# A new order of operations for the first two token chunks, with fixed buffer slots and two steps in halves

## The chip, the cores and the metric

One core of a Trainium2 chip runs the whole kernel. The core has a matrix engine (TensorE, PE in the views; its weight loads are PEld), VectorE (DVE), ScalarE (ACT), GpSimd (POOL), and SyncE (SP), whose queue issues all transfers between HBM and the on-chip memory SBUF. Matrix results go to PSUM, eight banks of 128 x 512 floats. The metric is the device time of one execution in microseconds.

## The reference, cut to what matters

Four sequences of 768 tokens, 8 heads of 64, all float32. Each query sees keys less than 16 positions away, and one summary for each block of 32 tokens (maximum of the keys, mean of the values). Its result is the input of a two-layer network.

```
k_sum = k.reshape(B, H, nb, 32, D).max(axis=3);  v_sum = v.reshape(B, H, nb, 32, D).mean(axis=3)
scores_l = scale * q @ k.T, -1e9 outside |i - j| < 16
scores_s = scale * q @ k_sum.T + log(32)
a = softmax(concat(scores_l, scores_s));  x = a @ concat(v, v_sum)      # 3072 tokens x 512
out = square(relu(x @ w_in)) @ w_out                                     # 512 -> 2048 -> 512
```

## The kernel before, in words

The 3072 tokens are 24 groups `g` of 128; two groups make a chunk `c`, so there are 12 chunks. The hidden width of 2048 is cut into 16 slices `f` of 128. For each chunk and slice, `ffn1` (L382) makes 12 matrix products of 256 columns: x and the weights are each split into a high and a low part, and three of the four pairs are multiplied. `ffn2` (L429) multiplies the squared result by the second weights, three products for each of two groups, 512 columns wide or as two of 256.

From chunk 2 on, the order is a plain loop (`slot`, `period`), in which the attention of the next chunk runs under the layers of this one. The change doesn't touch it. Chunks 0 and 1 are ordered by `START`, a list of tokens that stands in the file; one loop (L646 to L655) goes through it and issues each step to its engine's queue. Every engine works its queue in order. So the list sets, for each engine alone, what stands behind what, on SP too. The scheduler adds the semaphore waits that the data need, and no other freedom is left. The tokens that the prediction speaks of:

- `L:kv` (keys of sequence 0, for two heads each), `L:q`, `L:k`, `L:v`, `L:vn` (values for the means), `L:mask` (constants), `L:w` (weights, whole or a half): loads on SP.
- `KS` (L180): maximum over blocks of 32 keys, on DVE. `S` (L285, and L269 for groups 4 on): scores. `TT` (L297, DVE): mask and maximum of one head. `E` (L305, ACT): exponentials of one head. `NR`, `N` (L318, L325): sums, and division on POOL. `T` (L331, PE) and `TC` (L126): transposes of four heads, and their copy to SBUF.
- `SV` (L149, PE): block means of the values as products with a small matrix; `VC` (L126): copies of a quarter of them beside the loaded values, in the tiles `v_sb0` and `v_sb1`. `O` (L352): output of the attention. `XH`, `XL` (L366, L369): its high and low part.
- `HI`, `LO`, `SH`, `AD`, `CA`, `SU` (L229 to L254): turn a block of 64-bit weights into a high and a low float part, on ACT, DVE and POOL.
- `F1`, `F2`: a slice of the first layer; a slice of the second. `RE`, `SQ`, `MU`, `GL`: square of the relu and its low part. `Z` (L563): products of zeros whose result nobody reads.

Large blocks (keys, raw weights, split weights) lie in rooms of 32 KB per partition. Before, one pool of 18 rooms deals them out in turn:

```
def room(dtype, name):
    return big.tile([P, 8192 // mybir.dt.size(dtype)], dtype, name=name, tag="w", bufs=NF + SPARE)
```

Of the kernel before, what the change touches and what calls it, by code (L numbers as in the profile page):

```python
# [68 lines left out]
GL15v O5=4 VT3 F2.14.1 XH5 XL5
"""  # L70


# [1 line left out]
def attn_ffn_kernel(ctx: ExitStack, tc: tile.TileContext, q, k, kt, v, vt, v0, w, consts, out):  # L74
    nc = tc.nc
# [3 lines left out]
    big = ctx.enter_context(tc.tile_pool(name="big", bufs=1))  # L79
# [59 lines left out]
    def load_v(g):  # L139
        nc.sync.dma_start(out=v_sb[g % 2][0:96], in_=v[g // NT, g % NT])  # L140

    def sum_v0(vn):


        ps = ps_o.tile([P, DM], F32, name="o_ps")
        for t in range(NT):
            o = 20 - 4 * t
            for j in range(4):
                nc.tensor.matmul(  # L149
                    ps[j * 32 : j * 32 + 32, 0:P], lhsT=mean_sb[:, o : o + 32],  # L150
                    rhs=vn[t // 3][:, t % 3, j * P : (j + 1) * P], start=(t == 0), stop=(t == NT - 1),
                )
        return ps
# [10 lines left out]
    def load_kv0(p):  # L164


        if (p // 2) not in padded:
            padded[p // 2] = r = room(F32, "kv")[:, 0 : 2 * KPAD].rearrange("p (a k) -> p a k", a=2)
            nc.gpsimd.memset(r[:, :, 0:WINDOW], 0.0)
            nc.gpsimd.memset(r[:, :, KPAD - WINDOW :], 0.0)  # L170
        kv[0, p] = padded[p // 2][:, p % 2, WINDOW : WINDOW + S]
        nc.sync.dma_start(out=kv[0, p], in_=kt[0, p])

    def load_kv(b, p):
        kv[b, p] = r = room(F32, "kv")
# [70 lines left out]

    def high_w(f, j, eng):
        if f not in w_sb:
            w_sb[f] = room(F32R, "w_sb").rearrange("p (h c) -> p h c", h=2)
# [319 lines left out]
    def begin(op, i, j, eng, at, after):  # L569
# [167 lines left out]
```

## Time and profile before

| | us |
|---|---|
| runs shown | 606.45, 606.64 (median), 610.62 |
| the profiled execution | 607.6 |
| its span, from the first to the last instruction | 605.8 |
| PE busy, of the span | 593.8 |
| DVE, ACT, POOL busy | 386.0, 265.8, 105.2 |

The profiled execution took 1.8 us more than its span, and 1.0 us more than the median. The span is one timeline; "busy" is the time in which at least one instruction of the engine was under way. The groups of rows below are cut from the page of this execution and from answers on its trace; in a timeline row the first number is the start, the second the length of the merged piece, and brackets give the idle time before it and what ended it.

### The profile page before, as it was taken

What the parts mean: (1) busy time and instruction counts of PE and PEld (TensorE: products, weight loads), DVE (VectorE), ACT (ScalarE), POOL (GpSimd) and SP (SyncE); (2) the same over time, 40 slices, a digit from 0 to 9 for tenths busy, and PEclk for the clock granted to TensorE, in tenths of its full rate; (3) what the DMA queues carried; (4) which work ended last, traced back from release to release, by engine and by line L of the source; (5) the groups of instructions that cost most, each with busy time, mean ns of one, the idle gap of its engine ahead of it and who ended that gap; (6) DMA issues with size and microseconds to landing.
All of it is one profiled execution on the core that took longest, in us unless ns stands there. A gap on an engine that the chain in (4) does not pass through costs nothing.

```text
span 605.8 us, 14834 instructions
## 1 busy us (share of the span) xinstructions
PE 593.8 (98%) x6178; PEld 572.8 (95%) x6178; DVE 386.0 (64%) x1063; ACT 265.8 (44%) x687; POOL 105.2 (17%) x97
## 2 busy tenths in 40 slices
PE   7799999999999999999999999999999999999997
PEld 5689999999999999999999999999999999999997
DVE  5789899777637837847545855865663763663221
ACT  4888884334253432433425325425424434422222
POOL 3745755211100101102101101002101010110000
PEclk9999999999999999999999999999999999999999
DMA  8999571350007006006005204202201400200000
GB/s 274 328 363 417 204 260 56 112 168 35 1 11 269 2 2 226 2 2 226 2 1 199 81 2 131 97 2 87 88 2 38 139 2 2 88 1 2 36 1 35
DMA packets 19890, 60.46 MB, mean 100 GB/s; under 512 B 2288, under 2 KB 2288, under 8 KB 18288
## 3 DMA queue, kind: packets, MB, share of 16 engines
q1 hardware_dynamic: 19824, 59.53, 28.0%
q8 instruction: 48, 0.79, 0.6%
q14 instruction: 18, 0.15, 0.1%
HBM read 53.23 MB, written 6.29 MB: 98 GB/s over the span
## 4 chain that ended last, share of the span: by engine, by line
PE 95%; DMA 3%; DVE 1%; ACT 0%; issue 0%; SPq 0%
PE o_ps L429 43%; PE ph L382 39%; PE s_ps L382 4%; PE ph L352 4%; PE s_ps L269 3%; DMA v_sb<-in_v 1%; DMA q_sb<-in_q 1%; DMA kv<-in_kt 1%; DVE v_sb L126 1%; PE s_ps L285 0%; PE o_ps L149 0%; PE o_ps L563 0%; PE ph L331 0%; PE ph L285 0%; PE s_ps L352 0%
## 5 line engine op out<-in xcount | busy, mean ns | idle before, releaser
L382 PE MATMUL ph<-xh,w_sb 128*128 128x256 f32 x1376 | 241.2, 278 | 0.5 <-DVE xl L369 0.5
L429 PE MATMUL o_ps<-w_sb,gh 128*128 128x256 f32 (+1 forms) x1428 | 237.5, 285 | 0.0
L382 PEld LDWEIGHTS ph<-xh,w_sb 128*128 128x128 f32 x1376 | 213.3, 188 | 8.7 <-issue 1.3
L429 PEld LDWEIGHTS o_ps<-w_sb,gh 128*128 128x128 f32 x1428 | 191.0, 188 | 0.5 <-issue 0.3
L382 PE MATMUL ph<-xl,w_sb 128*128 128x256 f32 x688 | 190.5, 277 | 0.0
L429 PE MATMUL o_ps<-w_sb,gl 128*128 128x256 f32 (+1 forms) x670 | 150.5, 294 | 0.0
L401 DVE TENSOR_TENSOR ph<-ph,r 128x512 f32<-128x512 f32 x85 | 59.3, 699 | 141.5 <-ACT r L390 140.7
L390 ACT ACTIVATE r<-ph 128x512 f32<-128x512 f32 x84 | 49.9, 594 | 189.3 <-PE ph L382 189.3
L382 PEld LDWEIGHTS ph<-xl,w_sb 128*128 128x128 f32 x688 | 129.2, 188 | 0.0
L338 DVE STREAM_TRANSPOSE pT<-e_sb 32x256 f32<-32x256 f32 x240 | 104.6, 436 | 4.1 <-POOL e_sb L325 0.7
L305 ACT ACTIVATE e_sb<-e_sb,nmx 128x120 f32<-128x120 f32 x192 | 73.7, 386 | 75.5 <-DVE nmx L297 75.5
L429 PEld LDWEIGHTS o_ps<-w_sb,gl 128*128 128x128 f32 x670 | 104.6, 188 | 0.4
L325 POOL TENSOR_TENSOR e_sb<-e_sb,total 128x480 f32<-128x480 f32 x47 | 46.2, 991 | 322.1 <-DVE total L319 150.4
L396 ACT ACTIVATE gh<-r 128x512 fp32r<-128x512 f32 x94 | 59.5, 633 | 12.1 <-PE o_ps L429 6.5
L404 DVE TENSOR_TENSOR gl<-ph,gh 128x512 fp32r<-128x512 f32 x85 | 58.8, 692 | 9.2 <-DVE ph L401 0.5
L297 DVE CUSTOM_DVE_ANT_0 e_sb<-s_ps,consts_sb 128x120 f32<-128x120 f32 x180 | 40.7, 277 | 1.9 <-PE ph L331 1.1
L245 POOL TENSOR_TENSOR w_raw<-w_raw 128x1024 int32<-128x1024 int32 (+1 forms) x20 | 35.9, 1800 | 24.7 <-DVE w_raw L234 8.6
L305 ACT ACTIVATION_READ_ACCUMULATOR e_sb<-e_sb,nmx 128x1 f32 x192 | 36.3, 189 | 0.0
L369 DVE TENSOR_TENSOR xl<-ph,xh 128x512 fp32r<-128x512 f32 x22 | 15.2, 691 | 23.3 <-ACT xh L366 23.2
L382 PE MATMUL s_ps<-xh,w_sb 128*128 128x256 f32 x160 | 28.6, 279 | 0.0
L366 ACT CAST xh<-ph 128x512 fp32r<-128x512 f32 x22 | 12.9, 586 | 33.1 <-PE ph L352 33.1
L352 PEld LDWEIGHTS ph<-pT,v_sb 128*64 128x64 f32 x704 | 21.7, 138 | 5.2 <-issue 3.8
(79 smaller groups left out, 412.5 us busy)
## 6 DMA issues: line engine op xcount, KB each, us to landing
w_raw<-in_w SPq DMA_DIRECT2D x12, 1024.0 KB, 13.1
v_sb<-in_v SPq DMA_DIRECT2D x24, 384.0 KB, 4.4
k_sb<-in_k SPq DMA_DIRECT2D x20, 384.0 KB, 6.1
q_sb<-in_q SPq DMA_DIRECT2D x24, 256.0 KB, 5.5
kv<-in_kt SPq DMA_DIRECT2D x16, 384.0 KB, 5.9
out<-ob SPq DMA_DIRECT2D x24, 256.0 KB, 2.0
kv<-in_vt SPq DMA_DIRECT2D x12, 384.0 KB, 6.4
w_raw<-in_w SPq DMA_DIRECT2D x8, 512.0 KB, 8.3
```

Source lines behind the costliest of these rows:

```text
L245: nc.gpsimd.tensor_tensor(out=lo, in0=hi, in1=lo, op=ALU.add)
L297: nc.vector.tensor_tensor_reduce(out=e_sb(g)[:, h, 0:NK], in0=s_ps[g, half][h % 2][:, h // 2, 0:NK], in1=m, scale=-scale, scalar=3.0e38, o ...
L305: nc.scalar.activation(e, e, AF.Exp, bias=nmx[g, half][:, i : i + 1], scale=-1.0, accum_out=sm[g, half][:, i, 0:1])
L325: eng.tensor_mul(out=e, in0=e, in1=sm.pop((g, half)).unsqueeze(2).to_broadcast([P, 4, NK]))
L338: nc.vector.transpose(out=pT[g % 2][j * 32 : j * 32 + 32, :, i * 32 : i * 32 + 32], in_=e_sb(g)[i * 32 : i * 32 + 32, :, j * 32 : j * 32 + ...
L352: nc.tensor.matmul(xp[o : o + 64, h // 2, s * 64 : s * 64 + 64], lhsT=v_sb[g % 2][:, s, h * 64 : h * 64 + 64], rhs=pT[g % 2][:, h, s * 64 ...
L382: nc.tensor.matmul(ph, lhsT=w_sb[f][:, w, cc * P : (cc + 1) * P], rhs=x[c][:, cc, :], start=(n == 0), stop=(n == 3 * NC4 - 1))
L390: nc.scalar.activation(r, ph, AF.Relu)
L396: nc.scalar.activation(gh, r, AF.Square)
L401: nc.vector.tensor_mul(out=ph, in0=ph, in1=r)
L404: nc.vector.tensor_sub(out=gl, in0=ph, in1=gh.bitcast(F32))
L429: nc.tensor.matmul(o_ps[c][tt][:, o : o + step], lhsT=g_[:, ts_], rhs=w_sb[f][:, w, DM + o : DM + o + step], start=start and o == 0, stop= ...
```

## The change

`START` is another list of much the same tokens, 508 for 506. Every room has its own name now, and tables of numbers say which block lies in which. The constants are loaded in two parts: the masks of the first two kinds (`L:mask`), and later the third mask, the identity and the small matrix of the means (`L:rest`). `SV` is cut into `SV0` and `SV1`, one for each of the two loads that it reads.

```diff
+RAW_ROOM = (3, 2, 6, 9, 12, 14, 16, 17, 0, 1, 12, 7, 0, 3, 12, 7)
+W_ROOM = (5, 4, 10, 11, 13, 15, 8, 9, 2, 6, 16, 1, 17, 0, 3, 12)
+KV0_ROOM, VN_ROOM, KV_FIRST, KV_ROOM = (0, 1), (7, 8), (14, 14, 7, 17), (7, 14)
...
 START = """
-Z15 XT L:q0 L:kv0 L:kv1 KS0 L:kv3 KS1 L:kv2 KS3 S0.0=01 Z6 L:mask KS2 TT0.3 S0.1=23 TT0.1 L:q1 TT0.0 L:w0.1 L:w1.1
...
+L:kv0 Z15 Z6 L:q0 L:kv1 KS1 KS0 S0.0=01 L:kv3 KS3 L:kv2 KS2 L:mask TT0.2 TT0.0 E0.2 E0.0 TT0.3 E0.3 L:q1 PK5v S0.1=23
...
-    def sum_v0(vn):
-
-
-        ps = ps_o.tile([P, DM], F32, name="o_ps")
-        for t in range(NT):
+    def sum_v0(vn, n, ps):
+        if n == 0:
+            ps = ps_o.tile([P, DM], F32, name="o_ps")
+        for t in range(n * NT // 2, (n + 1) * NT // 2):
...
-    def room(dtype, name):
-
-        return big.tile([P, 8192 // mybir.dt.size(dtype)], dtype, name=name, tag="w", bufs=NF + SPARE)
+    def room(dtype, name, n):
+
+        return big.tile([P, 8192 // mybir.dt.size(dtype)], dtype, name=name, tag=f"room{n}")
...
-            w_raw[f] = room(I64, "w_raw")
+            w_raw[f] = room(I64, "w_raw", RAW_ROOM[f])
...
-            nc.sync.dma_start(out=consts_sb, in_=consts)
+            nc.sync.dma_start(out=consts_sb[:, 0 : 2 * NK], in_=consts[:, 0 : 2 * NK])
+        elif what == "rest":
+            nc.sync.dma_start(out=consts_sb[:, 2 * NK :], in_=consts[:, 2 * NK :])
...
-            v_mean[0] = sum_v0([vn[0], vn[1]])
+            v_mean[0] = sum_v0(vn, i, v_mean.get(0))
```

Counted over both lists, the list has as many zero products as before (32), three `LO` more on ACT and three fewer on DVE, three `CA` the other way round, one `SU` more on DVE and one fewer on POOL, two `RE` more on ACT and two fewer on DVE. Five more slices of the second layer stand directly ahead of another, and are therefore issued as twelve products of 256 columns instead of eight of 256 and two of 512.

The order on three engines, at the places that the prediction speaks of. First PE, between the second pair of transposes of group 1 and the first slice of the first layer; L331 are the transposes (e_sb_77 is that of the even groups), L149 the means, L269 the scores of group 4, L352 the outputs of groups 1 and 0. Before:

```order
L331 MATMUL ph<-consts_sb,e_sb_78 128x128 x4
L563 MATMUL o_ps<-zero 128x512
L331 MATMUL ph<-consts_sb,e_sb_77 128x128 x4
L149 MATMUL o_ps<-vn,consts_sb 32x128 x24
L563 MATMUL o_ps<-zero 128x512
L269 MATMUL s_ps<-k_sb_71,q_sb_75 64x120 x16
L352 MATMUL ph<-pT_80,v_sb_74 64x64 x16
L352 MATMUL s_ps<-pT_79,v_sb_73 64x64 x16
L331 MATMUL s_ps<-consts_sb,e_sb_77 128x128 x4
L331 MATMUL ph<-consts_sb,e_sb_78 128x128 x8
L382 MATMUL s_ps<-xh,w_sb 128x256 x2
```

And of the change (two lines of source further down):

```order
L333 MATMUL ph<-consts_sb,e_sb_78 128x128 x4
L151 MATMUL o_ps<-vn,consts_sb 32x128 x24
L333 MATMUL ph<-consts_sb,e_sb_77 128x128 x4
L354 MATMUL ph<-pT_80,v_sb_74 64x64 x16
L354 MATMUL s_ps<-pT_79,v_sb_73 64x64 x16
L333 MATMUL s_ps<-consts_sb,e_sb_77 128x128 x4
L333 MATMUL ph<-consts_sb,e_sb_78 128x128 x8
L271 MATMUL s_ps<-k_sb_71,q_sb_75 64x120 x16
L384 MATMUL s_ps<-xh,w_sb 128x256 x2
```

The means have moved ahead of the last transposes of group 0, the two zero products are gone from here, and the scores of group 4 stand behind the outputs, where they stood ahead of them.

Second, the copies of the means into `v_sb`. Before, all eight stand together on DVE (L126), behind the sums (L318, L319) of one set of heads and ahead of the sums of another. The change's rows on DVE:

```order
L321 RECIPROCAL total<-total 128x4
L129 COPY v_sb_73<-o_ps 32x2x128
L129 COPY v_sb_74<-o_ps 32x2x128
L129 COPY v_sb_73<-o_ps 32x2x128
L129 COPY v_sb_74<-o_ps 32x2x128
L299 ISA e_sb_77,nmx<-s_ps,consts_sb 128x120
```

and on ACT, with the semaphores that they wait for:

```order
L129 COPY v_sb_73<-o_ps 32x2x128 [waits PE_49]
L129 COPY v_sb_74<-o_ps 32x2x128
L307 ACTIVATE e_sb_78,sm<-e_sb_78,nmx 128x120 [waits DVE_49]
L129 COPY v_sb_73<-o_ps 32x2x128 [waits DVE_49]
L129 COPY v_sb_74<-o_ps 32x2x128
L307 ACTIVATE e_sb_78,sm<-e_sb_78,nmx 128x120
```

Half of the copies have moved to ACT, and the second pair there waits for DVE's first pair; DVE's pairs wait for ACT's in the same way (`VC2a VC0v VC3a VC1v` in the list), so the four pairs follow each other across two engines.

Third, the first loads on SP. Before:

```order
L130 DMA q_sb_75<-in_q 128x512
L172 DMA kv<-in_kt 128x768 x4
L549 DMA consts_sb<-in_consts 128x540
L130 DMA q_sb_76<-in_q 128x512
L218 DMA w_raw<-in_w 128x512 x2
L130 DMA q_sb_75<-in_q 128x512
L218 DMA w_raw<-in_w 128x512
L130 DMA q_sb_76<-in_q 128x512
L547 DMA vn<-in_v 128x1536 x2
```

And of the change:

```order
L174 DMA kv<-in_kt 128x768
L133 DMA q_sb_75<-in_q 128x512
L174 DMA kv<-in_kt 128x768 x3
L551 DMA consts_sb<-in_consts 128x240
L133 DMA q_sb_76<-in_q 128x512
L220 DMA w_raw<-in_w 128x512 x2
L133 DMA q_sb_75<-in_q 128x512
L553 DMA consts_sb<-in_consts 128x300
L133 DMA q_sb_76<-in_q 128x512
L220 DMA w_raw<-in_w 128x512
L549 DMA vn<-in_v 128x1536 x2
```

One load of keys goes ahead of the first queries, and the second part of the constants stands between two loads of queries. On DVE the list puts the reduction of the second pair of heads (`KS1`) ahead of that of the first (`KS0`), which came first before.

## Rows read from the trace of the kernel before

**Rows 1.** The page, parts 1 and 2: PE over the span, granted clock by slice.

```profile
PE 593.8 (98%) x6178; PEld 572.8 (95%) x6178; DVE 386.0 (64%) x1063; ACT 265.8 (44%) x687; POOL 105.2 (17%) x97
...
PEclk9999999999999999999999999999999999999999
```

**Rows 2.** Windows: stretch, its length, busy us by engine, clock, DMA share, GB/s.

```profile
6.00:37.80 31.80, 24.97 (x538) 20.63 (x537) 25.94 (x118) 22.96 (x83) 16.12 (x15) 1.00 0.98 324
30.00:37.80 7.80, 6.76 (x101) 5.97 (x98) 6.99 (x16) 6.29 (x12) 4.59 (x5) 1.00 0.97 306
37.80:60.00 22.20, 22.20 (x206) 21.33 (x203) 20.61 (x47) 19.92 (x29) 11.29 (x7) 1.00 1.02 417
```

**Rows 3.** Waits of PE from 40 us on: us in total, times, longest.

```profile
PE ph L382 <- DVE xl L369: 0.5, 1, 0.5
```

**Rows 4.** Chain that ended last, first 40 us: start, us, what held it.

```profile
1.63 5.60 DMA kv<-in_kt
...
29.46 7.22 DMA v_sb<-in_v
```

**Rows 5.** PE timeline to 38 us: start, us, instructions, idle before and releaser.

```profile
1.18 4.92 PE L563 MATMUL o_ps<-zero 128*128 128x512 f32 x15 [1.18 <-DVE zero L116]
...
18.05 0.40 PE L285 MATMUL s_ps<-kv,q_sb 64*64 64x96 f32 x8 [0.88 <-DMA q_sb<-in_q]
...
21.44 0.63 PE L331 MATMUL ph<-consts_sb,e_sb 128*128 128x128 f32 x4 [0.39 <-DVE pT L126]
21.99 1.51 PE L149 MATMUL o_ps<-vn,consts_sb 128*32 128x128 f32 x46
23.85 0.41 PE L149 MATMUL o_ps<-vn,consts_sb 128*32 128x128 f32 x2 [0.34 <-issue]
25.21 1.05 PE L269 MATMUL s_ps<-k_sb,q_sb 64*64 64x120 f32 x32 [0.54 <-DMA k_sb<-in_k]
...
27.44 0.92 PE L352 MATMUL ph<-pT,v_sb 128*64 128x64 f32 x24 [0.26 <-DVE v_sb L126]
...
33.59 0.33 PE L331 MATMUL ph<-consts_sb,e_sb 128*128 128x128 f32 x1 [0.78 <-issue]
...
36.72 1.15 PE L352 MATMUL ph<-pT,v_sb 128*64 128x64 f32 x32 [0.20 <-DMA v_sb<-in_v]
37.80 0.50 PE L382 MATMUL ph<-xh,w_sb 128*128 128x256 f32 x2
```

**Rows 6.** PE timeline, a piece of the second layer and the instruction behind it.

```profile
45.45 0.40 PE L429 MATMUL o_ps<-w_sb,gl 128*128 128x256 f32 x2
45.69 0.63 PE L429 MATMUL o_ps<-w_sb,gh 128*128 128x256 f32 x3
46.16 0.40 PE L429 MATMUL o_ps<-w_sb,gl 128*128 128x512 f32 x1
46.40 0.40 PE L382 MATMUL ph<-xh,w_sb 128*128 128x256 f32 x2
```

**Rows 7.** DVE timeline: reductions of the keys, first mask step, the mean's copies.

```profile
4.44 0.95 DVE L180 TENSOR_REDUCE ksum<-kv 128x24 f32<-128x768 f32 x1 [3.33 <-DMA kv<-in_kt]
7.25 2.90 DVE L180 TENSOR_REDUCE ksum<-kv 128x24 f32<-128x768 f32 x3 [1.86 <-DMA kv<-in_kt]
10.07 0.27 DVE L297 CUSTOM_DVE_ANT_0 e_sb<-s_ps,consts_sb 128x120 f32<-128x120 f32 x1
...
24.29 3.10 DVE L126 COPY v_sb<-o_ps 32x256 f32<-32x256 f32 x8 [0.69 <-PE o_ps L149]
```

**Rows 8.** ACT timeline: one exponential.

```profile
24.42 0.39 ACT L305 ACTIVATE e_sb<-e_sb,nmx 128x120 f32<-128x120 f32 x1
```

**Rows 9.** DVE timeline: the same subtraction twice.

```profile
73.61 2.92 DVE L254 TENSOR_TENSOR w_sb<-w_raw,w_sb 128x1024 fp32r<-128x1024 f32 x1
...
78.11 1.22 DVE L254 TENSOR_TENSOR w_sb<-w_raw,w_sb 128x1024 fp32r<-128x1024 f32 x1
```

**Rows 10.** POOL timeline at the first of them.

```profile
73.16 2.27 POOL L245 TENSOR_TENSOR w_raw<-w_raw 128x1024 int32<-128x1024 int32 x1 [2.03 <-DVE s_ps L401]
```

More of the change, by code (lines that the diff above doesn't have):

```diff
@@ L69 @@
-GL15v O5=4 VT3 F2.14.1 XH5 XL5
+L:kv0 Z15 Z6 L:q0 L:kv1 KS1 KS0 S0.0=01 L:kv3 KS3 L:kv2 KS2 L:mask TT0.2 TT0.0 E0.2 E0.0 TT0.3 E0.3 L:q1 PK5v S0.1=23
+S1.1=45 TT1.7 TT1.6 E1.6 XT L:w1.1 TT1.5 TT0.1 S1.0=45 TT1.0 PK4v TT1.4 L:w0.1 LO0.1v HI1.1 TT0.6 Z5 SH1.1 CA1.1v E1.0
+E0.1 NR0.0 TT1.2 TT1.1 Z2 N0.0p E1.4 TT0.4 Z2 L:q2 S2.0=12 HI0.1 TT1.3 SH0.1 LO1.1v E1.2 L:rest E1.5 T0.0=0 TT0.7 E1.3
+TT2.3 TT0.5 AD0.1 E1.1 NR1.0 Z1 E1.7 E0.6 Z1 TT2.1 N1.0p T1.0=4 TT2.0 TC0.0v S2.1=12 E0.5 NR1.1 E2.3 L:q3 CA0.1v E0.7
@@ new lines @@
+S3.0=30 TT2.2 TC1.0v TT3.0 TT3.2 L:w2.1 LO2.1a E2.0 HI2.1 N1.1p SH2.1 S3.1=30 E0.4 T1.1=5 L:vn0 E2.2 AD2.1 SV0 L:vn1
+E3.2 SV1 TT3.3 NR0.1 N0.1p T0.1=4 TT3.5 E2.1 E3.0 TT3.4 E3.3 TT3.1 E3.1 TT3.7 E3.4 E3.7 TT3.6 TC1.1v L:v1 NR2.0 VC2a
+VC0v E3.6 VC3a VC1v TT2.4 E3.5 TT2.6 E2.6 O1=5 L:v0 NR3.0 SU0.1p XH1 TC0.1v NR3.1 TT2.5 E2.5 TT2.7 O0=1 XH0 XL1 N2.0p
+T2.0=2 TC2.0a N3.0p T3.0=4 N3.1p T3.1=5 E2.4 XL0 L:k4 L:q4 S4.0=03 L:w3.1 S4.1=03 F1.0.0=1 E2.7 L:v3 AD1.1 SU1.1v
+NR2.1 CA2.1a N2.1p TT4.0 LO3.1a TT4.2 F1.0.1 SU2.1p TC3.0a T2.1=4 HI3.1 SH3.1 CA3.1v AD3.1 RE0v TC3.1a TC2.1a E4.0 SQ0
@@ new lines @@
+O3=2 L:w3.2 HI3.2 XH3 F1.1.0=4 MU0 GL0v TT4.4 TT4.1 LO3.2a TT4.6 SH3.2 XL3 L:v2 O2=5 XH2 SU3.1p XL2 CA3.2a F1.1.1
+L:w0.2 F1.3.0=5 F1.3.1 AD3.2 SU3.2v HI0.2 SH0.2 CA0.2v F1.2.0=2 L:w2.2 L:w1.2 L:w4 LO0.2a LO2.2a F1.2.1 HI2.2 SH2.2
+RE1v HI1.2 SH1.2 CA2.2a AD0.2 SU0.2v AD2.2 LO1.2a F2.0.0 L:k5 E4.1 SQ1 AD1.2 MU1 GL1v CA1.2a SU1.2v SU2.2v L:q5
+S5.1=14 S5.0=14 HI4 SH4 LO4a AD4 TT4.5 TT5.0 TT5.1 TT4.3 RE2v MU2 CA4a E5.0 SU4v L:w5 HI5 F2.0.1 F2.1.0 F2.1.1 SH5
+CA5v LO5a AD5 L:w6 EV0.0v F1.4.0=0 F1.6.0=3 TT5.3 L:q6 SQ2 GL2v EV0.1a HI6 E4.4 SH6 SU5v E5.1 F2.2.0 F2.2.1 L:w7 LO7v
@@ new lines @@
+LO6a HI7 SH7 AD7 RE3a SQ3 TT4.7 E4.6 MU3 TT5.7 GL3v L:w8 HI8 L:w9 L:w11 E5.7 L:q7 F1.4.1 RE4v TT5.4 SQ4 TT5.5 CA6a MU4
+GL4v F1.6.1 E5.4 LO9v AD6 SU6v F2.3.0 F2.3.1 CA7a SU7v F2.4.0 F2.4.1 E4.5 L:w13 TT5.6 TT5.2 HI9 SH9 SH8 LO8a AD8 E5.6
+E4.7 CA8a F1.5.0=2 F1.5.1 RE5v E5.2 RE6a MU5 SQ5 GL5v F1.7.0=5 CA9a L:k7 L:w10 F1.7.1 AD9 MU6 SU8v LO11a SU9v LO10v
+HI10 SH10 F2.5.0 F1.8.0=0 RE7a F1.8.1 HI11 SH11 AD11 E4.2 SQ6 E4.3 GL6v L:kw0 KT0 NR4.0 L:v4 MU7 F2.5.1 EV1.1v EV1.0a
+CA10a L:kw3 VT3 SQ7 L:w12 KT3 AD10 SU10v F1.12.0=1 F1.12.1 GL7p HI13 L:v5 CA11a SU11v SH13 NR4.1 N4.1p LO12a VT0 HI12
@@ new lines @@
+SH12 CA12a RE8v MU8 N4.0p TU4.1 F2.6.0 F2.6.1 SQ8 F2.7.0 F2.7.1 GL8v F1.13.0=2 L:w14 F1.9.0=5 AD12 SU12p HI14 LO13a
+F1.9.1 TU4.0 RE9a MU9 AD13 E5.5 L:w15 SH14 LO14a AD14 L:kw1 CA13a SU13v SQ9 HI15 GL9v KT1 F1.13.1 SH15 CA14a SU14v
+F2.8.0 F2.8.1 F1.14.0=3 F1.10.0=4 F1.10.1 RE10a L:k6 LO15a AD15 E5.3 F1.14.1 F2.9.0 TU4.2 CA15a SU15v SQ10 F2.9.1
+F1.11.0=0 F1.11.1 MU10 RE12a GL10v O4=4 L:kw2 F2.10.0 F2.10.1 RE11v SQ11 MU11 GL11v F2.11.0 NR5.0 N5.0p F2.11.1 KT2
+PK6a NR5.1 RE13a SQ12 MU12 GL12p F1.15.0=5 XH4 EV2.0v F1.15.1 EV2.1v MU13 XL4 N5.1v TU5.1 F2.12.0 SQ13 TU5.0 F2.12.1
@@ L70 @@
+GL13p RE15a MU15 PK7a F2.13.0 F2.13.1 S6.0=01 RE14a SQ14 MU14 SQ15 S7.1=23 S7.0=23 S6.1=01 TU5.2 O5=4 GL14p F2.14.0
+F2.14.1 XH5 VT2 XL5 VT1 GL15v
 """
@@ L174, in load_kv @@
     def load_kv(b, p):
-        kv[b, p] = r = room(F32, "kv")
+        kv[b, p] = r = room(F32, "kv", KV_FIRST[p] if b == 1 else KV_ROOM[p % 2])
         nc.sync.dma_start(out=r[:, 0:S], in_=kt[b, p])
@@ L248, in high_w @@
         if f not in w_sb:
[L249 removed]
+            w_sb[f] = room(F32R, "w_sb", W_ROOM[f]).rearrange("p (h c) -> p h c", h=2)
         copy(eng, w_sb[f][:, 0, part(j)], words(f, j)[1].bitcast(F32))
```

28 lines of the change are left out of this document (2 added, 26 removed).

## The prediction, made before the change was run

> **What bounds the kernel now.** I read the page first. PE is busy 593.8 of 605.8 us and its clock is granted in full in all 40 slices [rows 1]. So nothing can be won by faster neighbours except where PE stands idle, which leaves 12.0 us to find. The windows say where. From 37.80 us on PE has no gap: in the stretch from 37.80 to 60 it is busy 22.20 of 22.20 us [rows 2], and in the waits after 40 us the whole rest of the run shows one, of 0.5 us [rows 3]. From 6.00 to 37.80 PE is busy 24.97 of 31.80, so 6.83 us are idle there [rows 2]; the remaining idle time lies ahead of 6 us, where products of zeros run until the first keys come. The first slice of the first layer, at 37.80 [rows 5], is therefore the milestone (in the change the outputs of group 2, at 36.72 before, stand behind that slice; I count them as work in front of it on both sides): what the change does to the work in front of it (the same work on both sides) goes one for one into the time, and what comes behind it is PE at full load, unless the change opens a gap there.
>
> The chain of waits that ended last begins with the fourth load (keys, from 1.63, landed 7.23) and holds, late, the load of values from 29.46 to 36.68 [rows 4]. Between them the chain hops through all engines. In PE's timeline the reader is to see who released it at each step: transposes at 21.44 waited 0.39 for DVE; the means follow at 21.99; the outputs at 27.44 waited for DVE's copies of those means; the outputs of group 2 at 36.72 waited 0.20 for values. Two pieces waited for nothing that the profile shows, 0.34 at 23.85 and 0.78 at 33.59, marked "issue" [rows 5]. The DMA engines' busy share is 0.98 between 6.00 and 37.80 and 1.02 behind it [rows 2], so one that is put ahead pushes back another.
>
> The sum is made against the profiled execution of 607.6, which is 1.0 above the median of the runs shown, 606.6; I subtract that 1.0 at the end.
>
> **The change part by part.**
>
> *Reductions of the keys, +0.95.* Before, KS0 ran alone at 4.44 for 0.95, in time in which DVE had to wait for keys anyway, and the three others took 2.90 from 7.25, when the later keys landed; the first mask step came at 10.07 [rows 7]. Now KS0 stands behind KS1, whose keys are a later load. DVE works in order, so KS0 falls behind that wait and four stand in a row: the first mask step comes one reduction later, 0.95. If KS1's keys land early, because one load of keys now goes ahead of the queries, nothing is lost. Bounds 0 and +0.95; I take the upper one, as 7.25 is what the row shows for a landing, and the mask steps then feed exponentials, division and transposes one by one.
>
> *Zero products, 0.* There are 32 before and after, 21 of them now at the start. Fifteen took 4.92 us from 1.18 [rows 5], so six more last about 2 us and are over before the four reductions, on which the first scores' masks wait.
>
> *Constants in halves, 0.* Their first part is smaller, but the mask step stands behind KS2 on DVE, which the keys hold, not behind the constants: at 10.07 it follows the reductions with no wait [rows 7]. The second part stands ahead of one load of queries on SP; there PE waited for queries, 0.88 at 18.05 [rows 5]. The same columns are moved in all, the others of them later, so the queries behind them lose what those ahead win. I cost it at nothing.
>
> *Means ahead of the last transposes, -0.94.* PE reached the transposes at 21.44 after 0.39 of waiting, so was free at 21.05. The means began at 21.99 [rows 5]. They wait for no transposes, so they can start at 21.05: 0.94 earlier. Bounds: all of it, or 0 when the values that they read have not landed. No row shows them late, so I take all.
>
> *Copies of the means on two engines, +0.5.* Eight copies in a row took 3.10 on DVE [rows 7], 0.39 each. Now four pairs alternate, ACT, DVE, ACT, DVE, and each waits for the one before, so they do not run beside each other: the 3.10 stays, and three handovers come on top. ACT has an exponential between its pairs, 0.39 [rows 8], beside DVE's pair. A handover from DVE's copy to PE shows as 0.26 [rows 5]. Three of these are 0.8; with the whole exponential in the way 1.2; without any loss 0. I take 0.5, between. DVE is free for two pairs meanwhile, but its next steps wait for products too.
>
> *Scores of group 4, +1.05.* Before, they stood under the copies: PE did them from 25.21 for 1.05 [rows 5], while it would have waited for the copies. Now they stand behind the outputs and transposes, where PE has other work queued, so their 1.05 is on the path, and the place that they filled is idle. Bounds +0.5, if half falls in a gap such as the 0.78 at 33.59, and +1.05, which I take.
>
> *Stalls that go, -1.32.* The 0.20 for values should go, as their loads stand earlier in the list; the two issue gaps lie where PE's program happens to stand, and other instructions stand there now: 0.34 + 0.78 + 0.20 = 1.32 [rows 5]. I take all of it; the other end is -0.30, with a gap of the same kind elsewhere. These gaps are a behaviour of fetching as far as a row can tell: no semaphore ends them. The Trainium skill, *Runtime: NRT & Kernel Launch*, section "Instruction fetch mechanics", says that an engine's program streams in by blocks and that the cost of crossing into the next is mostly hidden. The trace does not bear that out if these gaps are such crossings, 0.34 and 0.78; by the page they would be something else that the change need not remove, and the sum would be 1.12 higher.
>
> *Halved slices of the second layer, 0.* Two products of 256 columns take 0.24 from start to start (45.45 to 45.69), one of 512 takes 0.24 (46.16 to 46.40) [rows 6]. What moves between ACT, DVE and POOL behind 37.80 (three `LO`, three `CA`, one `SU`, two `RE`) is hidden under PE, which shows no gap there; the rooms by table change no duration.
>
> The sum: 0.95 - 0.94 + 0.50 + 1.05 - 1.32 = +0.24, so 607.8 for an execution like the profiled one and **606.8** beside the median. With all low ends (0 - 0.94 + 0 + 0.50 - 1.32 = -1.76) it is 604.9; with all high ends (0.95 + 0 + 1.2 + 1.05 - 0.30 = +2.90) 609.5.
>
> **The rivals.**
>
> *Faster.* The new order may close the gaps in front of the milestone, since every engine's place in line is different. For it speaks that 6.83 us of idle are there and that PE's waits go to many releasers, so one list can serve several. Against it: the loads are at their share throughout, and the keys' landing and the chain through five engines stay. Half of the idle time is 3.4: 606.6 - 3.4 = 603.2. More than 1% (6.1 us) would need nearly all of it.
>
> *Slower, by the clock.* The zero products and the scores that stood between the transposes at 21.44 and the outputs at 27.44 are gone from there. PE then has the means and one set of transposes, and idles until the copies are through, about three pairs of copies, 2.3 us, and more with handovers. The longest idle time before, 0.88 at 18.05 [rows 5], left the granted clock at 1.00 (of 2.4 GHz) in every stretch [rows 2]; nothing shows what a longer one does. If it falls to 1.2 GHz for the products that follow, PE's 6.76 us between 30.00 and 37.80 [rows 2] double at worst, +6.8, or half of them do, +3.4: 606.8 + 3.4 = 610.2 up to 613.6. It decides as soon as the copies start late. The Trainium skill, *TensorE: Matmul & The Clock Gate*, section "HAM oscillation — how this bites in real kernels", has idle gaps of a matmul loop put the engine back to its low clock, so that the next products start cold; it speaks against this change, and the trace of before, with gaps below 0.9 us and a full clock, has no case of it.
>
> *Slower, by thin cover.* Behind 37.80 DVE is busy 20.61 of 22.20 us and ACT 19.92 [rows 2]. The same subtraction on DVE took 2.92 at 73.61 and 1.22 at 78.11; at the first, POOL ran an operation of 2.27 from 73.16 [rows 9, 10]. Such a meeting costs 1.7; if the new order puts one or two where DVE is nearly full, PE waits for it: 606.8 + 1.7 to 3.4 = 608.5 to 610.2.
>
> *No effect.* If a load (the values at 36.68) sets the milestone whatever stands before it, 606.6; this lies in my own range.
>
> **How the numbers follow.** The sum, with no effect, 0.62; faster 0.14; the clock 0.14; thin cover 0.10. The range has to reach into three rivals: 604.2 leaves out the better half of the faster one (0.07), 610.8 the worse part of the clock (0.09), and it takes in 604.9 to 609.5. About 1%, 6.1 us, is what a measurement of this kernel can tell from no change. Faster than 600.5 needs nearly all of the idle time: 0.04. Slower than 612.7 needs most of the clock rival's price, or two rivals together: 0.07. The rest, 0.89, lies within 1%.
>
> **What would show it.** The milestone (first slice with the last outputs) should stand within 38.0 plus or minus 2 us, and PE have no gap behind it. The first mask step should stand near 11.0; the means near 21 to 22; the copies should take 3.1 to 4.3 us from first to last, with PE idle under them for over 2 us; the scores of group 4 should take 1.05 with PE busy on both sides; the gaps marked "issue" should be gone from the means and the transposes. A clock below 1.00 in any stretch, or a wait of PE behind 40 us of more than 1 us, would make the prediction wrong; so would a first mask step ahead of 10 us.

## The result, and the profile after

| | before | the change |
|---|---|---|
| median of 20 runs, us | 606.41 | 610.44 |
| lowest and highest | 605.15 to 610.62 | 607.24 to 615.02 |
| the profiled execution, and its span | 607.6, 605.8 | 609.51, 607.4 |
| ratio, 95% interval | | 1.0069 [1.0055, 1.0083] |

The change is slower by about 4 us, 0.7%. That lies inside the range (604.2 to 610.8) and within 1%, but it is not what the likeliest case said (606.8): it is the rival "slower, by the clock" (610.2 to 613.6). One execution of a variant below (`s4_q4`) ran at a granted clock of 0.56 throughout and took 994.94 us; it is left out of that variant's median, and its trace is the only one of that variant. On the page of the change, TensorE and the clock:

```profile
PE 595.8 (98%) x6188; PEld 576.4 (95%) x6188; DVE 381.1 (63%) x1058; ACT 268.8 (44%) x693; POOL 100.4 (17%) x96
...
PEclk8999999999999999999999999999999999999999
```

PE is busy for 2.0 us more than in [rows 1], though it does no more work worth the name; the first digit of the clock row is 8 where it was 9. Windows show where (the columns are those of [rows 2]):

```profile
6.00:11.90 5.90, 4.44 (x111) 3.55 (x109) 5.10 (x18) 1.44 (x7) 0.00 (x0) 1.00 0.99 363
11.90:15.30 3.40, 3.40 (x37) 2.95 (x36) 2.17 (x14) 2.74 (x11) 0.00 (x0) 0.50 0.51 167
15.30:28.95 13.65, 8.66 (x208) 6.69 (x207) 10.20 (x57) 11.11 (x49) 8.36 (x8) 1.00 0.93 303
28.95:32.37 3.42, 3.42 (x62) 3.30 (x61) 2.45 (x14) 1.65 (x6) 2.66 (x3) 0.50 0.28 67
32.37:60.00 27.63, 27.63 (x321) 26.21 (x320) 22.94 (x54) 24.44 (x47) 14.03 (x11) 1.00 1.02 393
```

Twice, from 11.90 and from 28.95, the granted clock is 0.50 of 2.4 GHz for 3.4 us, with PE busy all through; elsewhere from 6 us on it is full. PE's timeline at the places that the prediction spoke of, to be held against [rows 5]:

```profile
13.06 3.31 PE L567 MATMUL o_ps<-zero 128*128 128x512 f32 x9
16.30 0.40 PE L287 MATMUL s_ps<-kv,q_sb 64*64 64x96 f32 x8
...
19.79 0.65 PE L333 MATMUL ph<-consts_sb,e_sb 128*128 128x128 f32 x4 [1.70 <-POOL e_sb L327]
...
23.81 1.52 PE L151 MATMUL o_ps<-vn,consts_sb 128*32 128x128 f32 x48
25.25 0.33 PE L333 MATMUL ph<-consts_sb,e_sb 128*128 128x128 f32 x1
27.49 0.49 PE L333 MATMUL ph<-consts_sb,e_sb 128*128 128x128 f32 x3 [1.91 <-issue]
27.91 0.34 PE L354 MATMUL ph<-pT,v_sb 128*64 128x64 f32 x4
28.78 1.65 PE L354 MATMUL ph<-pT,v_sb 128*64 128x64 f32 x28 [0.54 <-DVE v_sb L129]
30.21 1.93 PE L354 MATMUL s_ps<-pT,v_sb 128*64 128x64 f32 x32
...
33.66 1.05 PE L271 MATMUL s_ps<-k_sb,q_sb 64*64 64x120 f32 x32
34.64 0.51 PE L384 MATMUL s_ps<-xh,w_sb 128*128 128x256 f32 x2
...
39.10 0.51 PE L384 MATMUL ph<-xh,w_sb 128*128 128x256 f32 x2
...
40.67 1.15 PE L354 MATMUL ph<-pT,v_sb 128*64 128x64 f32 x32
```

In the first stretch nine products of zeros take 3.31 us, and the scores of group 2 stand behind them. Ahead of the second PE does next to nothing for three microseconds: a pause of 1.91 that no semaphore ends, seven short products, then 0.54 of waiting for the copies. What follows runs at half speed: the outputs of group 0 took 1.93 here, where 32 such products took 1.15 in [rows 5]. DVE's and ACT's timelines, for [rows 7]:

```profile
6.19 3.53 DVE L182 TENSOR_REDUCE ksum<-kv 128x24 f32<-128x768 f32 x4 [5.07 <-DMA kv<-in_kt]
9.64 0.27 DVE L299 CUSTOM_DVE_ANT_0 e_sb<-s_ps,consts_sb 128x120 f32<-128x120 f32 x1
...
13.17 0.28 DVE L299 CUSTOM_DVE_ANT_0 e_sb<-ph,consts_sb 128x120 f32<-128x120 f32 x1 [1.16 <-PE ph L287]
...
15.75 0.28 DVE L299 CUSTOM_DVE_ANT_0 e_sb<-s_ps,consts_sb 128x120 f32<-128x120 f32 x1
...
26.52 0.75 DVE L129 COPY v_sb<-o_ps 32x256 f32<-32x256 f32 x2 [0.66 <-ACT v_sb L129]
27.97 0.75 DVE L129 COPY v_sb<-o_ps 32x256 f32<-32x256 f32 x2 [0.70 <-ACT v_sb L129]
```

```profile
25.86 0.63 ACT L129 COPY v_sb<-o_ps 32x256 f32<-32x256 f32 x2
26.52 0.39 ACT L307 ACTIVATE e_sb<-e_sb,nmx 128x120 f32<-128x120 f32 x1
...
27.31 0.63 ACT L129 COPY v_sb<-o_ps 32x256 f32<-32x256 f32 x2 [0.30 <-DVE v_sb L129]
```

Behind 40 us PE waits as it did in [rows 3]:

```profile
PE ph L384 <- DVE xl L371: 0.5, 1, 0.5
```

So PE loses nothing behind it. The prediction's milestone, 37.80, is the start of the second slice of the first layer, not of the first slice (30.83 before, 34.64 in the change). It came at 39.10, and with the 1.08 of the outputs of group 2, which now stand behind it (40.67), at 40.2: 2.4 later than before. Part of that is won back further on. Adding up PE's rows from start to start, up to the same product (the 4,700th from the end, at 136.56 us before and 138.22 after; from there both take 469 us), gives the +1.66 between the two profiled executions by kind of work:

```
outputs +1.19   scores of groups 0 to 3 +0.92   zeros +0.73   transposes +0.65
idle -0.38      means -0.40                     scores of group 4 on -0.23   both layers -0.83
```

PE's idle time did not grow. The four kinds that ran in the two stretches (the first line) grew by 3.5. The two stretches hold 6.8 us of PE's work at half speed, so about 3.4 us of PE's time are the clock's, and all else together fell by 1.7. Two single executions don't bear more than that: the profiled one of before is 1.2 above its kernel's median, that of the change 0.9 below its own. The mean granted clock of each of the 20 runs of the change sorts them:

```
granted clock   runs   us
1.000           2      607.24, 607.74
0.997           1      608.79
0.993, 0.994    12     609.51 to 611.35
0.992, 0.988    2      612.69, 612.76
0.986           3      613.13 to 615.02
```

A stretch of 3.4 us at half clock lowers the mean over 607 us by 3.4 x 0.5 / 607 = 0.003. A mean of 0.999 is a full clock up to PE's last product: in the trace of before the only stretch at 0.50 begins at 604.77, behind it. From row to row the time grows by about 1.4 us for each such stretch, and the typical run has two. That makes some 2.9 of the 4.0 us; about 1 is left at full clock. The kernel before falls too, which its one trace, at full clock, could not show: of all its runs beside the experiments below, 60 have 0.999 or 1.000 (median 606.2) and 26 less (606.8), nearly all of these one stretch. So a fall is rarer there, and by these medians it costs less. These are correlations; the experiments intervene.

### The profile page after: what moved, and what is told of

It is laid out like the page before. It is cut to its first block, busy times and chain, and to the rows that moved or that the text cites. A ratio compares the mean times of both kernels' runs of the same rounds, so it can differ in the third digit from the quotient of the medians.

```text
span 607.4 us, 14853 instructions
## 1 busy us (share of the span) xinstructions
PE 595.8 (98%) x6188; PEld 576.4 (95%) x6188; DVE 381.1 (63%) x1058; ACT 268.8 (44%) x693; POOL 100.4 (17%) x96
## 4 chain that ended last, share of the span: by engine, by line
PE 96%; DVE 1%; DMA 1%; ACT 1%; issue 0%; POOL 0%; SPq 0%; POOLq 0%; DVEq 0%
PE o_ps L431 43%; PE ph L384 39%; PE s_ps L384 5%; PE ph L354 4%; PE s_ps L271 3%; DMA kv<-in_kt 1%; DVE ksum L182 1%; PE o_ps L567 1%; PE s_ps L287 0%; PE s_ps L354 0%; PE ph L333 0%; DVE e_sb L299 0%; PE ph L287 0%; DVE v_sb L129 0%; PE s_ps L333 0%
## 5 line engine op out<-in xcount | busy, mean ns | idle before, releaser
L247 POOL TENSOR_TENSOR w_raw<-w_raw 128x1024 int32<-128x1024 int32 (+1 forms) x20 | 33.1, 1661 | 28.5 <-DVE w_raw L242 17.1
```

The lines of the kernel that those rows point to most:

```text
L247: nc.gpsimd.tensor_tensor(out=lo, in0=hi, in1=lo, op=ALU.add)
```

## The experiments

Theory A: the granted clock. Theory B: the order itself, a longer chain over the copies. Theory C (later): the scores of group 4, whose 1.05 us lost their cover. Each kernel was timed in turn with the kernel before on one chip. Four chips served, on which the kernel before had medians of 606.51 (`zeros_early`, `zeros_long`, `zeros_both`, `before_no_zeros`), 606.00 (`zeros_stall`, `s4_back`, `s4_stall`, `copies_dve`), 606.10 (`after_again`, `before_s4_late`, `s4_q4`) and 606.91 (`before_copies`). So kernels of different groups are compared by their ratios to the kernel before, or by their distance from it, not by their times.

**Five zero products moved forward, `zeros_early`.**

```diff
-L:kv0 Z15 Z6 ... PK5v S0.1=23 ... TT0.1 S1.0=45 ... TT0.6 Z5 SH1.1
+L:kv0 Z15 Z4 ... PK5v Z2 S0.1=23 ... TT0.1 Z3 S1.0=45 ... TT0.6 Z2 SH1.1
```

> The changed kernel with five of its zero products moved into PE's waits: two fewer at the start and three fewer ahead of the scores of group 2, two more ahead of the second scores of group 0 and three more ahead of those of group 1. Theory A (the granted clock): the changed kernel lost time because PE, idle in pieces between 8 and 12 us, was granted half its clock from 11.9 us, and again from 29.0; with the first piece of idle time filled the first fall becomes rarer. It put the nine zeros at 13.06 on the chain at 3.24 us where 2.0 would do, so 1.2 us come back: 609.2, mean granted clock 0.997 instead of 0.994. Theory B (the order): the time went to the longer chain over ACT and DVE in the copies, and the clock only stretches work that waits in any case: 610.4, within 0.4.

Measured: 608.79, ratio 1.0035 [1.0020, 1.0050], below the change's interval. Five of twelve runs had a clock of 1.000 (608.08 to 608.61), six 0.997 (608.71 to 609.86). Theory A gave 609.2; B's 610.4 is out. By the runs the gain is the clock's: at full clock this kernel is no faster than the change (607.24 and 607.74), but more of its runs have it. In its trace the first stretch is gone, the second stands:

```profile
11.90:15.30 3.40, 2.25 (x32) 1.59 (x29) 3.00 (x21) 2.89 (x11) 0.60 (x1) 1.00 0.63 214
15.30:27.90 12.60, 7.61 (x204) 6.07 (x203) 9.36 (x51) 10.55 (x46) 7.76 (x8) 1.00 0.88 306
27.90:31.40 3.50, 3.50 (x62) 3.38 (x58) 2.34 (x12) 1.93 (x6) 2.85 (x3) 0.51 0.33 82
```

The timelines of PE and DVE show what the first stretch had cost:

```profile
12.12 1.58 PE L567 MATMUL o_ps<-zero 128*128 128x512 f32 x6
...
15.15 0.31 PE L287 MATMUL s_ps<-kv,q_sb 64*64 64x96 f32 x3 [1.15 <-DVE nmx L299]
```

```profile
12.23 0.28 DVE L299 CUSTOM_DVE_ANT_0 e_sb<-ph,consts_sb 128x120 f32<-128x120 f32 x1 [0.65 <-PE ph L287]
...
14.81 0.28 DVE L299 CUSTOM_DVE_ANT_0 e_sb<-s_ps,consts_sb 128x120 f32<-128x120 f32 x1
```

DVE waited 0.65 for the scores of group 1, where it waited 1.16 at half clock. The scores of group 2, with fewer zeros ahead of them, did not simply come earlier: they waited for the mask step that ended at 15.09. In the change the same step ended at 16.03 and the scores began at 16.30. So in the profiled execution some 0.5 us of the first stretch lay in the scores of group 1 and some 0.2 in the zeros.

**Slower zeros under the copies, `zeros_long`, `zeros_both` and `zeros_stall`.** Products of the float32 zeros stand ahead of the last transposes of group 0.

```diff
+        elif op == "ZL":
+            for _ in range(i):
+                nc.tensor.matmul(z_ps[0], lhsT=zero32.to_broadcast([P, P]), rhs=zero32.to_broadcast([P, DM]), start=True, stop=True)
-NR1.0 Z1 E1.7 E0.6 Z1 TT2.1 ... N0.1p T0.1=4
+NR1.0 E1.7 E0.6 TT2.1 ... N0.1p ZL3 T0.1=4
```

That is `zeros_long`; `zeros_both` has the moves of `zeros_early` too, and `zeros_stall` these:

```diff
-Z15 Z6 ... S0.1=23 ... S1.0=45 ... Z5 SH1.1 ... Z2 L:q2 ... T0.1=4
+Z15 Z2 ... Z1 S0.1=23 ... Z3 S1.0=45 ... Z2 SH1.1 ... Z1 L:q2 ... ZL4 T0.1=4
```

> The changed kernel with three float32 zero products (slower ones, of more passes) between the means and the last transposes, where PE idles under the copies, and two single zeros behind the scores of group 2 taken out. Theory A (the granted clock): the second fall, at 29.0 us, becomes rarer; what followed it (outputs and transposes, 28.8 to 32.4) ran at half clock for 3.4 us with PE always busy, so 1.7 us come back: 608.7, mean granted clock 0.997. Theory B (the order): 610.4, or up to 0.7 more where the zeros hold up the outputs.

> Both edits on zero products together. Theory A (the granted clock): 1.2 and 1.7 us come back, 607.5, granted clock 1.00 in most runs; what is left over the kernel before, about 1.1, is the order's own price (forecast: 0.2). Theory B (the order): 610.4 to 611.

> As the kernel with five zero products moved forward (608.8 us), and four float32 zeros stand between the means and the last transposes, taken from the start and from behind the scores of group 1, so that 32 products of zeros stand ahead of the same 349th product as in the change, behind which PE paused 1.9 us for no event. PE should be busy from 25 to 27 us under the copies. Theory A (the granted clock): the second half-clock stretch, from 28 to 31 us, goes too, and its 1.7 us: 607.1, granted clock 1.00 in most runs. Theory B (the order): no change, 608.8, since the copies end when they did.

Measured: 610.96 (1.0072 [1.0049, 1.0095]), 610.73 (1.0055 [1.0034, 1.0077]) and 610.84 (1.0082 [1.0061, 1.0103]). All three missed A's numbers, and A gets no support from them as kernels. The first two lie in B's ranges (610.4 to 611.1 and 610.4 to 611), but their times go with the granted clock (in `zeros_long` from 607.75 at 0.999 to 613.63 at 0.986), which B does not have; the third missed B's 608.8 too. The first two took two zeros from ahead of the transposes at 19.8, and PE's wait there grew from 1.70 to 2.14; the stretches at half clock moved (11.4 to 18.3 and 21.7 to 28.5 in the one trace, 19.4 to 22.8 in the other) rather than went. In the third, the profiled run had a full clock and 608.49, the five others 0.991 to 0.997 and 610.71 to 612.91. Its PE timeline says why even the full clock won nothing:

```profile
24.80 2.42 PE L649 MATMUL o_ps<-zero 128*128 128x512 f32 x5
27.43 1.45 PE L649 MATMUL o_ps<-zero 128*128 128x512 f32 x3 [0.22 <-issue]
...
29.25 1.15 PE L354 MATMUL ph<-pT,v_sb 128*64 128x64 f32 x32
```

Four products became eight instructions and ended at 28.88, past the copies (28.27), so the outputs came at 29.25. A fill that outlasts its wait costs what it saves.

**The scores of group 4 back under the copies, `s4_back`,** on top of `zeros_early`.

```diff
-SV0 L:vn1 ... L:v1 NR2.0 VC2a VC0v ... XL0 L:k4 L:q4 S4.0=03 L:w3.1 S4.1=03 F1.0.0=1
+SV0 L:vn1 L:k4 ... L:v1 L:q4 NR2.0 VC2a S4.0=03 S4.1=03 VC0v ... XL0 L:w3.1 F1.0.0=1
```

> As the kernel with five zero products moved forward (608.8 us), with the scores of group 4 back under the copies of the means, and their keys' load ahead of the values', their queries' between the two values'. Theory C (the scores' own 1.05 us lie on the path, as forecast): 607.7 at least, with PE busy in 1 us more under the copies. With theory A (the granted clock) the second half-clock stretch becomes rarer besides, as PE idles less there: 606.0 to 607.0. If neither holds (the values land late and the outputs wait for them instead): 608.8 or up to 1 more.

Measured: 607.30, ratio 1.0021 [1.0006, 1.0037], against 1.0035 [1.0020, 1.0050] without: the intervals overlap. The edit did not put the scores where they were meant to lie. Their queries landed at 27.09, when the copies (24.59 to 27.46) were nearly over, and the scores held the outputs until 28.16; without them the outputs could have begun at 27.46. So about 0.35 of the 1.05 could come back. At full clock, the seven runs (median 606.97) are 1.4 above those of the kernel before beside them (605.54), where `zeros_early` was 1.8 above (608.24 against 606.44): 0.4 less. C is neither shown nor refuted by it. A holds in part: seven of twelve runs had 0.999 or 1.000, five without the edit, and its trace has a stretch at half clock again, from 28.2. PE:

```profile
25.75 0.49 PE L333 MATMUL ph<-consts_sb,e_sb 128*128 128x128 f32 x3 [1.44 <-issue]
27.18 1.05 PE L271 MATMUL s_ps<-k_sb,q_sb 64*64 64x120 f32 x32 [0.94 <-issue]
28.16 1.94 PE L354 MATMUL ph<-pT,v_sb 128*64 128x64 f32 x32
```

**Its queries earlier, `s4_q4`; both fills, `s4_stall`.** `s4_q4` puts `L:q4` ahead of `L:v1`; `s4_stall` is `zeros_stall` with the edit of `s4_back`.

> As the kernel that has the scores of group 4 back under the copies (607.3 us, 606.9 at full clock), with the queries of group 4 loaded ahead of both loads of values instead of between them: in its trace these queries landed at 27.09 us and the scores began at 27.18, held the outputs up to 28.16, while the copies had ended at 27.46. Landing about 25.5, they let the outputs begin at 27.5: 0.7 less, 606.6. If the values then land too late for the outputs: 607.3 to 608.

> Both the four float32 zeros under the copies and the scores of group 4 there. Theories A and C together: 606.0, granted clock 1.00 in most runs. B (the order): 608.8.

Measured: `s4_q4` 607.25 (median of eleven runs), ratio 1.0024 [1.0004, 1.0044], which is not told from 1.0021. Its seven runs at full clock (median 606.80) are 1.0 above those of the kernel before beside them (605.84), 0.5 less than `s4_back`, for 0.7 expected; with so few runs that is not clear of noise. In its one trace the queries landed at 26.97, not near 25.5, yet all of the scores (29.62 to 31.19) lay under the copies (28.95 to 31.81), which came late there. `s4_stall` 609.61, ratio 1.0067 [1.0041, 1.0093]: a miss for A and C together and for B. In its trace the zeros ended at 30.82, past the copies (30.12), and the scores began behind them, at 31.19.

**The copies on DVE, `copies_dve`,** on top of `zeros_early`: `VC2v VC0v ... VC3v VC1v`.

> As the kernel with five zero products moved forward (608.8 us), with all copies of the means on DVE again. Forecast (three handovers and an exponential between cost 0.5): the copies take 3.1 us in a row and end 0.5 earlier: 608.3. Rival, from the trace of the changed kernel, where the four pairs took 2.88 from first to last: 608.8 to 609.1; or up to 1.2 less, if the first copies no longer wait for the exponentials that stand ahead of them on ACT.

Measured: 609.41, ratio 1.0054 [1.0033, 1.0076], which overlaps 1.0035 [1.0020, 1.0050]: unclear. The row is clear (2.87 in `zeros_early`):

```profile
25.46 3.10 DVE L129 COPY v_sb<-o_ps 32x256 f32<-32x256 f32 x8
```

**One part alone in the kernel before: the copies, `before_copies`.** `VC1a E2.5 VC0v VC3a ... VC2v`.

> The kernel before with another part of the change alone: the copies of the means alternate between ACT and DVE, with one exponential between the two pairs on ACT. So far, the time outside the span was 2.1 us in every run of the kernels with copies of the means on ACT, and 1.8 in every run of those that have them on DVE. If the copies on ACT bring that about, it is 2.1 here as well, though all else is the kernel before. Forecast for the span (three handovers and an exponential): 0.5 more; by the changed kernel's trace (2.88 us from first to last, where 3.10 stood): 0.2 less. Together 606.3 to 606.9 beside 606.1.

Measured: 606.78, ratio 0.9995 [0.9982, 1.0008]: nothing. The copies took 2.87 us from first to last, where 3.10 stood. Outside the span there were 1.87 to 1.95 us, not the 2.1 expected, and 1.73 to 1.82 in the runs of the kernel before beside it.

**One part alone: the scores of group 4, `before_s4_late`.**

```diff
-E3.6 S4.1=03 TT2.6 ... E2.2 S4.0=03 L:w3.1 ... T3.0=4 CA2.1a XL0
+E3.6 TT2.6 ... E2.2 L:w3.1 ... T3.0=4 S4.1=03 S4.0=03 CA2.1a XL0
```

> The kernel before with one part of the change alone: the scores of group 4 taken out from under the copies of the means and put behind the transposes of group 3's first heads. Theory C (their 1.05 us lie on the path now): 606.2 + 1.05 = 607.3 with a granted clock as before. Theory A (the granted clock) adds that PE, idle under the copies, is granted half its clock behind them in some runs: up to 608.7, and a granted clock lower than before's in the median. If the copies' stretch was no cover (the values' load at 28.2 us sets the outputs): 606.2 to 606.6.

Measured: 607.52, ratio 1.0024 [1.0005, 1.0043], or 0.3 to 2.6 us: inside what A and C gave, and only its low end touches the third reading (up to 0.5). None of the twelve runs reached a clock above 0.997; of the 23 runs of the kernel before beside them 14 had 1.000 and 2 had 0.999. The trace has both halves of the story, in PE's timeline and in the windows:

```profile
23.15 0.48 PE L563 MATMUL o_ps<-zero 128*128 128x512 f32 x1
26.83 1.55 PE L352 MATMUL ph<-pT,v_sb 128*64 128x64 f32 x32 [3.20 <-DVE total L319]
28.25 1.97 PE L352 MATMUL s_ps<-pT,v_sb 128*64 128x64 f32 x32
...
31.46 1.05 PE L269 MATMUL s_ps<-k_sb,q_sb 64*64 64x120 f32 x32
```

```profile
20.00:27.35 7.35, 3.31 (x71) 2.34 (x72) 6.55 (x36) 6.23 (x30) 4.96 (x6) 1.00 1.03 282
27.35:30.80 3.45, 3.45 (x57) 3.29 (x53) 1.09 (x4) 1.12 (x3) 2.65 (x3) 0.51 0.98 325
```

With its cover work gone, PE idles 3.20 us while the copies run (to 26.38) and the values land (26.70); the products behind run at half clock, and the scores follow, exposed, with their 1.05.

**Fewer zeros before, `before_no_zeros`:** the eleven products of the tokens `Z5`, `Z2`, `Z2`, `Z1`, `Z1` behind the scores of group 1 are gone.

> The kernel before without the eleven zero products that it issues behind the scores of group 1 and later (the 21 earlier ones stay); nobody reads their results. Theory A (the granted clock): PE is idle where they stood, one or two stretches at half clock appear between 11 and 30 us, and the kernel with less work is slower by 1.2 to 3.4 us: 607.6 to 609.8. Theory B (the order): less work in front of the milestone, 606.4 or up to 0.5 less.

Measured: 606.87, ratio 1.0003 [0.9984, 1.0022]: no difference. A missed its price (607.6 to 609.8), and this bounds it; B's 606.4 lies in the interval. No run had a clock above 0.997. In the trace it fell for 10.24 us without a break, and PE's timeline shows why that hardly cost anything:

```profile
18.70:29.00 10.30, 8.90 (x127) 7.27 (x127) 7.99 (x45) 6.44 (x31) 6.19 (x6) 0.50 1.02 308
```

```profile
25.20 1.88 PE L269 MATMUL s_ps<-k_sb,q_sb 64*64 64x120 f32 x32 [0.87 <-DMA k_sb<-in_k]
27.01 2.08 PE L352 MATMUL ph<-pT,v_sb 128*64 128x64 f32 x32
```

The scores of group 4 began at 25.20, as they did at 25.21 in [rows 5], because their keys landed then; they lay under the copies (24.40 to 27.50), and half a clock only used up time that PE would have waited. Behind them the pause of 0.78 and the wait of 0.20 for values in [rows 5] did not come, and the second slice began at 36.83, ahead of 37.80.

**The change again, `after_again`,** for a second trace.

> The changed kernel once more, on the chip of the two other kernels of this study, with a second trace. 610.4 by its own earlier runs. Theory A (the granted clock) has the time go by the granted clock of each run: about 607.5 where it was 1.000, some 1.4 us more for each step of 0.003; and the second trace shows the fall near 29 us again while PE has only outputs to do under the copies.

Measured: 611.18, ratio 1.0077 [1.0048, 1.0105]. Six runs, none at full clock, from 0.994 (610.03) to 0.988 (611.98); the slowest, 613.28, had 0.992. In its trace the clock was 0.50 from 11.0 to 17.9 and from 31.5 to 34.9, and the nine zeros took 4.01 us. There the second stretch begins with the outputs of group 0, again behind a pause of 1.98 for no semaphore, seven products and 0.47 of waiting for the copies.

No kernel beat the one before.

## Why the prediction was right, and where it was not

The time lies in the range only because the range reached into the clock's rival, which had 0.14; the forecast's own case, a full clock, was seen in 2 of 26 runs, at 607.2 to 607.7. Two of the signs that were to make the prediction wrong came: a clock below 1.00, and a first mask step ahead of 10 us (9.64, but 10.34 in the second trace). The milestone missed its 38.0 plus or minus 2 by 0.2. That the sum lay within 1 us of the full-clock runs is in part luck, as errors of both signs cancel in it. Of the 12.0 us of idle time that it set out from, 3.5 lie behind PE's last product (602.28), not ahead of 6 us, and could not be won. Step by step:

- **Reductions of the keys, +0.95: wrong.** The four ran in a row, as said, but from 6.19 instead of 7.25, and the first mask step came at 9.64 (10.34 in the second trace), not 11.0. The low end was nearer: -0.4 against 10.07, and +0.3 in the second trace. I took one trace's landing time for that load. It is the third on the queue on both sides (the prediction calls it the fourth), and it landed at 5.85 to 7.49 in the four traces whose first loads are those of before, at 5.63 to 6.87 in the ten with those of the change. Between executions it moves by more than the term.
- **Zero products, 0: wrong, some +0.2 to +0.9.** Costed at nothing because PE would wait anyway. At half clock the nine took 3.31 us, and the scores of group 2 stood behind them; at full clock six took 1.58 in `zeros_early`, so nine would take some 2.2. But the mask step that these scores wait for ended only 0.27 ahead of them in the profiled execution (16.03, 16.30), and 0.97 in the second trace (17.14, 18.11). Moving five zeros, by which the first fall became rarer, gained some 1.7 in all.
- **Means first, -0.94: wrong sign.** They began at 23.81, not 21.05; still 22.65 in `zeros_early`. They no longer wait for the last transposes, but the change puts them behind scores of group 3 that wait for mask steps, and transposes at 19.79 waited 1.70 for POOL's division. I moved the step along the old timeline, where everything ahead of it was early.
- **Constants in halves, 0: not separated.** PE waited for no queries any more, where it had waited 0.88 [rows 5].
- **Copies on two engines, +0.5: wrong, about 0.** 2.87 us in both traces where 3.10 stood, below the 3.1 to 4.3 expected; no difference in time as a part alone. The exponential ran beside DVE's pair.
- **Scores of group 4, +1.05: right by the rows.** Their row is 1.05, with PE busy on both sides. As a part alone, in `before_s4_late`, they cost 1.4 with the clock's share (0.3 to 2.6); putting them back was no clean test. What the term left out is that they kept PE at work under the copies: without them the clock fell, in `before_s4_late` too.
- **Stalls that go, -1.32: wrong in sum.** The wait for values and the pause of 0.78 are gone, but the pause of 0.34 did not go, it grew to 1.91: +0.6 of such idle time instead of -1.32. It stands behind the same, 349th, product of PE's program in the kernel before (0.34; 0.59 in `before_copies`), in the change (1.91 and 1.98), in `zeros_early` (2.02), `copies_dve` (1.73) and `s4_back` (1.44), whatever instruction comes next. The traces show what it is, a part of TensorE's program that was fetched late (last section). It lies under the copies and so costs little by itself, but nothing that is queued behind it can fill that time. The Trainium skill, *Runtime: NRT & Kernel Launch*, section "Instruction fetch mechanics", has the crossing of a block of instructions mostly hidden; the trace agrees for 46 or 47 of 48 blocks, and not for this one, a pause of 1.9.
- **The halved slices and the cover behind 37.80, 0: right.** The layers' rows even shrank by 0.83, and PE has the same single wait of 0.5.
- **The rivals.** Nothing collided behind 37.80, and the gaps in front were not closed. By the clock: the place was right (behind the quiet stretch at the copies), one of two; the condition was met (idle time longer than any before: 1.91 and 0.54 with seven products between, against 0.88), though the kernel before loses its clock in some runs without it; the price was not right. I priced one fall that lasts until 37.80, 3.4 to 6.8; here there were two of 3.4 us, worth about 1.4 each by the times of the runs. The Trainium skill, *TensorE: Matmul & The Clock Gate*, section "HAM oscillation — how this bites in real kernels", says that idle gaps in a stream of products start the next ones cold, and the traces agree (0.50 behind the gap, 1.93 for 1.15); they add that it costs only where PE is what others wait for.

What stays open: at full clock the change is some 1 us above the kernel before. The 1.05 of the scores would cover that, but no experiment shows it alone at full clock, and the terms that went up (means) and down (keys, layers) were not separated further. Nor was it found what decides over the first stretch at half clock: the change has it behind 1.46 us of idle time between 6.00 and 11.90, `zeros_early` had 0.51 there and none, but the profiled execution of before had 1.36 and none either.

## What to carry to other kernels

Work that fills a wait of TensorE had two prices here when it was moved: its own time where it landed, and the clock of what stood behind the wait that it left empty. So before moving cover work, add up what TensorE does in the microseconds around it, and ask whether what stands behind is waited for: if it is, half a clock is paid for; where loads were waited for instead (`before_no_zeros`), it cost nothing. A landing time or a full clock read from one trace is one draw: look at the spread of several before a term is built on it.

## What the runs showed that was not expected

The time outside the span was 2.04 to 2.16 us in every run of the change and its variants with copies of the means on ACT, 1.73 to 1.82 in `copies_dve`, 1.73 to 1.84 in the kernel before and its two variants without such copies, and 1.87 to 1.95 in `before_copies`, where only those copies moved. So a few copies placed early on ACT go with 0.1 to 0.3 us that no row of the span holds; how, stays open.

Each product of the float32 zeros ran as two instructions, eight for four, and five of the eight took 2.42 us at full clock; of the other form of zeros six took 1.58.

The pauses marked "issue" are fetches of instructions. The page of the change has one queue that moved 48 packets of 16 KB of instructions (first line below), one for about 259 of TensorE's 12,425 (products, weight loads and waits), and the two pauses of before stand 256 of its instructions apart. In the change such a packet was under way from 24.97 to 26.18 (second line, of a window from 24.9 to 26.2), PE ran out at 25.58 and went on at 27.49:

```profile
q8 instruction: 48, 0.79, 0.5%
q8 instruction: 1, 0.02, 5.8%
```

Each pause that is named here behind the 349th product, and the 0.78 of before, ended 1.3 to 1.6 us after the end of such a packet. Where the packet ended over 2 us ahead of PE's arrival at that place (20.57 and 22.94 in `before_s4_late`), there is no pause. Why the packet started at 24.97 in the change and at 21.52 in the kernel before stays open.
